# The product with w_spatial as a 2x2 block product of seven products

## Chip, cores and metric

One core of one Trainium2 chip runs the whole program. The metric is the device time of one execution in microseconds; the median of several runs is compared.

## The reference, cut to what matters

Local-plus-summary attention makes x (4 batches, 768 positions, 512 features). Then, per batch:

```python
h = np.maximum(x @ w_in, 0.0)                    # 512 -> 1024
u, v = h[..., :512], h[..., 512:]
v_n = (v - mean(v)) / sqrt(var(v) + 1e-6)        # over the 512 features
v_s = einsum('ts,bsd->btd', w_spatial, v_n) + b_spatial[None, :, None]   # 768 x 768 by 768 x 512
out = (u * v_s) @ w_out                          # 512 -> 512
```

## The kernel before

All products are float32 in three passes: every operand is split into a high and a low float32r part, and `mm3` (line 572) issues, for each block of 128 of the sum, high by high, high by low and low by high, all into one PSUM tile.

Per batch there are these stages, with the names that the profile shows. Attention: `s` (scores), softmax on VectorE (line 478) and ScalarE (482), sums of its rows (line 486) and their reciprocal, `t` (transposes), `x` (mix with v). `proj_v` (`pv`, six tiles of 128 positions; normalised, then split into `vnh` and `vnl`), `proj_u` (`pu`, eight tiles, kept in one `u` buffer), `spatial` (`sp`), `proj_out` (`po`, six tiles, out through `ob`). The attention of the next batch is laid between the dense stages of the present one.

`spatial(b, th, d)` makes one tile of the product: 128 features of v by 512 (`th` = 0) or 256 (`th` = 1) positions, six steps of `mm3`, so 18 matmuls. Then VectorE adds the bias `brep` out of PSUM (line 640), VectorE or GpSimd multiplies by `u` (641), the result is split into high and low (`gt`, `gu`; cast in line 268, subtraction in line 649). The split weight lies in `wsp_h` and `wsp_l` for the whole run, and `po` of four tiles comes between the `th` = 0 and `th` = 1 blocks.

Weights are loaded and split in the first 90 us. The u half of `w_in` has staging of its own: c = 0 and 1 in the place of `u`, c = 2 and 3 in quarters in the `g` places. `wsp_h` lies in the place `wsh`, after `vn`, which holds v of batch 0 for its block sums (`vsums`) and is read last by GpSimd's copy in line 418.

`Plan` gives each operation a place and an engine. An operation that lists several engines (`two_ns`: VectorE or GpSimd) gets one of them. `ORDER` is a written list of all operations with their engines, and each engine runs its part of the list in that order, SyncE's queue of transfers too (line 262). A transfer that waits for a place holds up all that stand behind it in that queue. Up to 110 us of the plan's time each GpSimd operation waits for the last VectorE operation marked `port` that stands before it in the list.

Of the kernel before, what the change touches and what calls it, by code (L numbers as in the profile page):

```python
# [9 lines left out]
F32 = mybir.dt.float32  # L10
# [29 lines left out]
NG = 10  # L40
# [154 lines left out]
def tile_local_summary_attention_gmlp(ctx: ExitStack, tc: tile.TileContext, qT, kext, vext, vnat, vT, w_in, w_sp, b_rep, w_out, out):  # L195
# [130 lines left out]
    def win_load(half, pri):  # L326
        fs = half * DF
        stages = {}
        for c in range(NC):
            if half == 0 and c >= U_BIG:  # L330
                for o in range(0, DF, TH):
                    st = Buf(moe, [P, 2 * TH], F32, "g", f"wi{half}_{c}_{o}")
                    f = Buf(moe, [P, DF], F32, "e", f"wf{half}_{c}_{o}")
                    cs = slice(fs + o, fs + o + TH)
                    split64(st, 0, f, 0, win_v[:, c, cs], win_h[:, c, cs], win_l[:, c, cs], pri, f"wi{half}_{c}_{o}")
                continue
            if c % 2 == 0:
                tag = ("u", None, "vnl", "vnh")[2 * half + c // 2]
                stages[c // 2] = Buf(big, [P, 3 * 1024], F32, tag, f"wi{half}_{c}")
            st = stages[c // 2]  # L340
# [407 lines left out]
    for b in range(B):  # L748
# [21 lines left out]
        for d in range(NC):  # L770
            piece(4.1, spatial, b, 0, d)
# [173 lines left out]
```

## Time and profile before

| | |
|---|---|
| median of 3 runs | 402.4 us (401.82 to 403.41) |
| profiled execution | 400.33 us, span of its core 398.6 us |
| granted TensorE clock, mean | 0.995 |
| PE busy | 388.1 us (97%), 3573 matmuls |
| DVE, ACT, POOL busy | 268.6 us (67%), 201.0 us (50%), 102.4 us (26%; 132 instructions) |
| moved by DMA | 46.36 MB, mean 116 GB/s |
| chain that ended last, by engine | PE 84%, DVE 5%, DMA 4%, ACT 3% |

PE is TensorE, PEld its weight load, DVE VectorE, ACT ScalarE, POOL GpSimd, SP SyncE. Times run from the start of the span. Matmuls are pipelined: the duration that a row shows for one is longer than its distance to the next.

### The profile page before, as it was taken

To read this page: it belongs to the slowest core of one execution; us is meant where nothing else is said; L and a number is where in the kernel's file an instruction comes from. 1 tells how busy PE (TensorE), PEld (TensorE's weight loads), DVE (VectorE), ACT (ScalarE), POOL (GpSimd) and SP (SyncE) were. 2 spreads that over 40 slices of the span, in tenths; PEclk is the share of its full clock that TensorE was granted. 3 is DMA by queue.
4 is the path that set the end of the run, shared out by engine and by line. 5 is a ranking of instruction groups with operands and counts; after the bars stand their busy time and mean duration, and the time that the engine had idled before them with its cause. 6 is when DMAs were issued, how large, how long until landed. Compare 5 with 4: busy or idle time off the path is not lost.

```text
span 398.6 us, 9455 instructions
## 1 busy us (share of the span) xinstructions
PE 388.1 (97%) x3573; PEld 329.6 (83%) x3573; DVE 268.6 (67%) x942; ACT 201.0 (50%) x668; POOL 102.4 (26%) x132
## 2 busy tenths in 40 slices
PE   8699999999999999999999999999999999999996
PEld 8377788887988888898888889888888888888895
DVE  3799999999894988794646657764873535626431
ACT  3599998498273575723615644453734351211101
POOL 4035564520300123222541103331140223300000
PEclk9899999999999999999999999999999999999999
DMA  7987898451334671513247423005012120000022
GB/s 263 398 267 192 277 272 246 140 152 45 95 113 110 238 209 56 146 37 104 76 121 254 109 87 73 2 27 126 10 28 80 40 68 30 0 2 0 0 81 79
DMA packets 22542, 46.36 MB, mean 116 GB/s; under 512 B 2656, under 2 KB 6752, under 8 KB 22368
## 3 DMA queue, kind: packets, MB, share of 16 engines
q1 hardware_dynamic: 22352, 45.62, 37.4%
q8 instruction: 28, 0.46, 0.5%
q14 instruction: 18, 0.15, 0.1%
q10 hardware_dynamic: 144, 0.13, 0.1%
HBM read 39.45 MB, written 6.29 MB: 115 GB/s over the span
## 4 chain that ended last, share of the span: by engine, by line
PE 84%; DVE 5%; DMA 4%; ACT 3%; POOL 1%; SPq 1%; issue 1%; POOLq 0%; ACTq 0%; DVEq 0%
PE sp L572 24%; PE pu L572 17%; PE pv L572 15%; PE po L572 15%; PE x L538 5%; PE s L465 5%; DMA qd<-in_qT_dram 3%; PE t L522 2%; DMA k<-in_kext_dram 1%; SPq L262 1%; ACT p L482 1%; DVE p L478 1%; ACT p L493 1%; PE t L514 1%; DVE gm L377 1%
## 5 line engine op out<-in xcount | busy, mean ns | idle before, releaser
L482 ACT ACTIVATE p<-p,sums 128x120 f32<-128x120 f32 x192 | 73.8, 386 | 45.9 <-DVE sums L478 45.5
L572 PE MATMUL sp<-wsp_h,vnh 128*128 128x512 f32 (+1 forms) x192 | 65.7, 342 | 0.1
L572 PE MATMUL sp<-wsp_l,vnh 128*128 128x512 f32 (+1 forms) x192 | 64.6, 337 | 0.0
L572 PE MATMUL sp<-wsp_h,vnl 128*128 128x512 f32 (+1 forms) x192 | 64.6, 336 | 0.0
L478 DVE CUSTOM_DVE_ANT_0 p<-s,mask 128x120 f32<-128x120 f32 x192 | 45.4, 275 | 22.4 <-PE s L465 22.1
L572 PE MATMUL po<-wo_h,gt 128*128 128x512 f32 (+1 forms) x136 | 47.9, 383 | 0.0
L572 PE MATMUL pu<-xh,win_h 128*128 128x256 f32 (+1 forms) x128 | 43.9, 343 | 0.0
L572 PE MATMUL pu<-xh,win_l 128*128 128x256 f32 (+1 forms) x128 | 43.1, 337 | 0.0
L572 PE MATMUL pu<-xl,win_h 128*128 128x256 f32 (+1 forms) x128 | 43.1, 336 | 0.0
L641 POOL TENSOR_TENSOR g<-g,u 128x256 f32<-128x256 f32 (+1 forms) x18 | 17.7, 992 | 89.7 <-DVE g L640 59.8
L572 PEld LDWEIGHTS sp<-wsp_h,vnh 128*128 128x128 f32 x192 | 36.4, 189 | 5.3 <-DVE ob L268 0.5
L572 PEld LDWEIGHTS sp<-wsp_h,vnl 128*128 128x128 f32 x192 | 36.4, 189 | 3.9
L572 PEld LDWEIGHTS sp<-wsp_l,vnh 128*128 128x128 f32 x192 | 36.4, 190 | 3.8
L572 PE MATMUL po<-wo_l,gt 128*128 128x512 f32 (+1 forms) x100 | 38.2, 382 | 0.0
L572 PE MATMUL pv<-win_h,xh 128*128 128x512 f32 x96 | 37.9, 395 | 0.0
L572 PE MATMUL pv<-win_l,xh 128*128 128x512 f32 x96 | 37.4, 390 | 0.0
L572 PE MATMUL pv<-win_h,xl 128*128 128x512 f32 x96 | 37.4, 390 | 0.0
L640 DVE TENSOR_TENSOR g<-sp,brep 128x512 f32<-128x512 f32 (+1 forms) x32 | 17.6, 554 | 29.2 <-PE sp L572 24.1
L482 ACT ACTIVATION_READ_ACCUMULATOR p<-p,sums 128x1 f32 x192 | 36.2, 189 | 0.0
L572 PEld LDWEIGHTS po<-wo_h,gt 128*128 128x128 f32 x136 | 25.1, 188 | 5.5 <-issue 0.5
L493 ACT ACTIVATE p<-p,sums 128x120 f32<-128x120 f32 x80 | 24.6, 384 | 8.6 <-DVE sums L488 8.5
L538 PEld LDWEIGHTS x<-pt,ve 120*64 120x64 f32 x768 | 23.6, 138 | 5.9 <-issue 3.2
(131 smaller groups left out, 776.0 us busy)
## 6 DMA issues: line engine op xcount, KB each, us to landing
k<-in_kext_dram SPq DMA_DIRECT2D x16, 544.0 KB, 5.6
qd<-in_qT_dram SPq DMA_DIRECT2D x24, 256.0 KB, 3.8
ve<-in_vext_dram SPq DMA_DIRECT2D x23, 256.0 KB, 4.2
out_dram<-ob SPq DMA_DIRECT2D x23, 256.0 KB, 2.1
vt<-in_vT_dram SPq DMA_DIRECT2D x24, 192.0 KB, 2.5
wi<-in_w_in_dram SPq DMA_DIRECT2D x6, 512.0 KB, 6.7
ve<-in_vext_dram SPq DMA_DIRECT2D x22, 128.0 KB, 3.1
wo<-in_w_out_dram SPq DMA_DIRECT2D x8, 256.0 KB, 3.7
```

The costliest lines, as they stand in the source:

```text
L262: add(("SP", issue), lambda e: nc.sync.dma_start(out=out_() if callable(out_) else out_, in_=in_() if callable(in_) else in_), pri, w, r, ...
L377: nc.vector.tensor_reduce(out=g[:, 4 * lo:4 * top].rearrange("p (s g) -> p s g", g=4), in_=t[:, lo * SEG:top * SEG].rearrange("p (s c) -> ...
L465: nc.tensor.matmul(out=ps.t[r * QB:(r + 1) * QB, a, i * KW:(i + 1) * KW], lhsT=qt[hs, r, i], rhs=kts[r].t[hs, g * SEG:g * SEG + KW], start ...
L478: add(("DVE", 203), lambda e, i=i, mi=mi: nc.vector.tensor_tensor_reduce(out=pt.t[:, i, :], in0=ps.t[:, a, i * KW:(i + 1) * KW], in1=mask[ ...
L482: add(("ACT", 380), lambda e, i=i: nc.scalar.activation(out=pt.t[:, i, :], in_=pt.t[:, i, :], func=AF.Exp, scale=-1.0, bias=st.t[:, 0, i:i ...
L493: nc.scalar.mul(out=pt.t[:, i, :], in_=pt.t[:, i, :], mul=st.t[:, 0, i:i + 1])
L514: nc.tensor.transpose(out=ps.t[:KW, a, i * P:(i + 1) * P], in_=pts[a].t[:, i, :], identity=ident)
L522: nc.tensor.transpose(out=ps.t[:KW, r, a * CH + i * QB:a * CH + (i + 1) * QB], in_=pts[a].t[hs, i, :], identity=ident[hs, hs])
L538: nc.tensor.matmul(out=ps.t[a * D:(a + 1) * D, r, n * QB:(n + 1) * QB], lhsT=win(buf, n, o), rhs=rhs(n, a, r), start=True, stop=True)
L572: nc.tensor.matmul(out=ps.t[:, :n], lhsT=x, rhs=y, start=(j == i == 0), stop=(j == last and i == 2))
L640: add(("DVE", dve_ns(n)), lambda e: nc.vector.tensor_add(out=g.t[:, :n], in0=ps.t[:, :n], in1=brep[:, ts]), pri, w=[g], r=[ps, "brep"])
L641: add(two_ns(n), lambda e: eng(e).tensor_mul(out=g.t[:, :n], in0=g.t[:, :n], in1=u.t[:, d, ts]), pri, w=[g], r=[u, (u, d, th)], port=True)
```

## The change

Batch 0 keeps its direct product, in tiles of 384 positions instead of 512 and 256. In batches 1 to 3 the weight and v are cut in 2x2 blocks (384 positions or 384 summed positions; 256 features), and the product is made from seven products of blocks and sums of blocks instead of eight products of blocks. `combine` makes the sums of v's blocks and splits them, with the block sums `z` going to `vs`, which lies in `wsh`. `wsp_mix` makes the sums of the weight's blocks once, after batch 0, from a second read of `w_sp`; they go to DRAM (`mixed_w`), as do the plain split blocks from batch 0 (`wsp_keep`, `plain`). `sums_of` issues the seven products; each reads its three chunks of split weight back from DRAM (`tr`) into one of six places `wl` and issues two tiles of 384 positions, nine matmuls each. VectorE adds each product to what it belongs to.

`u`, the sums, the gated tiles and the stages of weights share eleven places `q` of 768 words. The v means of a batch (`vmean`) are read in quarters instead of halves. The u half of `w_in` with c = 0 to 2 is staged in `wsh`, after `vn` and before `wsp_h`. The order of the last tiles is 3, 4, 5, 0, 1, 2. `ORDER` is written anew as a whole.

```diff
-NG = 10
+HALF = S // 2
+NP = NT // 2
+NQ = 11
+VT = 4
...
-    SLOTS = dict(wsh=1, wsl=1, st=2, ..., g=NG, e=3, u=1, vnh=1, vnl=1, ...)
+    SLOTS = dict(wsh=1, wl=NT, st=2, ..., q=NQ, e=3, vnh=1, vnl=1, ...)
...
+    wsp_l = [Buf(big, [P, S], F32R, "wl", f"wsl{c}") for c in range(NT)]
+    plain = dram.tile([3, NP, P, 2, HALF], F32, name="plain")
+    mixed_w = [dram.tile([2, NP, P, 2, HALF], F32, name=f"mixed_w{i}") for i in range(2)]
...
             if c % (2 if half else 3) == 0:
+                stages[0] = Buf(big, [P, 3 * 1024], F32, ("vnl", "vnh")[c // 2], ...) if half else Buf(big, [P, NT * S], F32, "wsh", ...)
...
+    def wsp_keep(c, pri):
+        p, odd = divmod(c, 2)
+        rows = slice(1, 3) if odd else slice(0, 1)
+        cols = S if odd else HALF
+        for w, src, key in ((0, lambda: wsp_h.t[:, c, :cols], [wsp_h]), (1, lambda: wsp_l[c].t[:, :cols], [wsp_l[c]])):
+            dma(plain[rows, p, :, w].rearrange("o q n -> q o n"), ..., cols / 2, pri, w=[f"wt{c}{w}"], ...)
+
+    def wsp_mix(p, pri):
+        r = []
+        for i in range(2):
+            st = Buf(moe, [P, 2, HALF], F32, "q", f"wx{p}_{i}")
+            dma(lambda st=st: st.t.rearrange("q o n -> q (o n)"), wsp_v[2 * p + i], 384, pri, w=[st], r=["db"], ...)
+            r.append(st)
+        for (o, oi), (x, xi), (y, yi) in (((0, 0), (0, 1), (0, 0)), ((0, 1), (1, 1), (0, 1)), ((1, 1), (1, 1), (0, 0)), ((1, 0), (1, 1), (1, 0))):
+            add(two_ns(HALF), lambda e, ...: eng(e).tensor_sub(out=r[o].t[:, oi], in0=r[x].t[:, xi], in1=r[y].t[:, yi]), ...)
+        for i in range(2):
+            h, l = [Buf(big, [P, 2, HALF], F32R, "wl", f"tg{p}_{i}{w}") for w in "hl"]
+            add(dict(ACT=act_ns(S), DVE=one_ns(S)), lambda e, i=i, h=h: copy(e, h.t, r[i].t), ...)
+            add(two_ns(S), lambda e, i=i, h=h, l=l: eng(e).tensor_sub(out=l.t, in0=r[i].t, in1=h.t), ...)
+            for w, src in enumerate((h, l)):
+                dma(mixed_w[i][:, p, :, w].rearrange("o q n -> q o n"), lambda src=src: src.t.bitcast(F32), 384, ...)
...
+    def combine(b, p, v0, v1, pri):
+        vh, vl, vs = s["vh"], s["vl"], s["vs"]
+        z = Buf(moe, [P, S], F32, "q", f"z{b}_{p}")
+        lo, hi = slice(0, TH), slice(TH, DF)
+        for out_, x, y, op in (((z, lo), (v0, lo), (v0, hi), ALU.subtract), ((v0, hi), (v0, hi), (v1, hi), ALU.add),
+                               ((z, hi), (v0, hi), (v0, lo), ALU.subtract), ((z, slice(DF, S)), (v1, lo), (z, hi), ALU.subtract)):
+            add(two_ns(TH), lambda e, ...: eng(e).tensor_tensor(...), ...)
+        for q, v in enumerate((v0, v1)):
+            divide(v, ..., DF, pri)
+        divide(z, lambda: z.t, ..., S, pri)
...
+    def sums_of(b, piece):
+        def product(n, j, src, o, out_, other, minus, pri, key=None):
+            chunks = []
+            for p in range(NP):
+                ch = Buf(big, [P, 2, HALF], F32R, "wl", f"tr{b}_{n}_{p}")
+                dma(lambda ch=ch: ch.t.bitcast(F32), src[o, p], 384, pri - 9, w=[ch], r=need, tag=f"tr{b}_{n}_{p}")
+                chunks.append(ch)
+            for i in range(2):
+                ps = Buf(ps_m, [P, 512], F32, "m", f"sp{b}_{n}_{i}")
+                mm3(ps, HALF, [...chunks[p].t[:, 0], chunks[p].t[:, 1]... for p in range(NP)], pri, ..., early=True)
+                add(("DVE", dve_ns(HALF)), add_up, pri, w=[(out_, i)], r=[ps, out_, ...])
+        step(3.14, lambda pri: product("1", 0, plain, 0, f1, bias(0), False, pri, brk))
+        step(3.14, lambda pri: (product("2", 2, plain, 1, c11, of(f1), ...), gate(b, 0, 0, c11, None, pri)))
+        step(3.14, lambda pri: product("6", 5, mixed_w[1], 1, f1, of(f1), ...))
+        step(3.14, lambda pri: product("7", 4, mixed_w[0], 1, u3, of(f1), ...))
+        step(3.14, lambda pri: (product("5", 1, mixed_w[0], 0, f5, bias(1), ...),
+                                both(f1, f1, f5, ...), both(f5, u3, f5, ...), gate(b, 1, 1, f5, None, pri)))
+        step(3.14, lambda pri: (product("3", 6, plain, 2, f1, of(f1), ...), gate(b, 0, 1, f1, 0, pri), gate(b, 0, 1, f1, 1, pri)))
+        step(3.14, lambda pri: (product("4", 3, mixed_w[1], 0, u3, of(u3), True, ...), gate(b, 1, 0, u3, 0, pri), gate(b, 1, 0, u3, 1, pri)))
...
-        for d in range(NC):
-            piece(4.1, spatial, b, 0, d)
-        for t in range(4):
-            piece(2.72, proj_out, b, t)
-        for d in range(NC):
-            piece(2.16, spatial, b, 1, d)
-        for t in range(4, NT):
+            for c in range(NT):
+                wsp_keep(c, KEEP_AT + c)
+        if b == 0:
+            for y in range(2):
+                for d in range(NC):
+                    piece(3.14, spatial, b, y, d)
+                for t in range(y * NP, y * NP + NP):
+                    piece(2.72, proj_out, b, t)
+            add(two_ns(HALF), lambda e: eng(e).tensor_sub(out=brep[:, HALF:], in0=brep[:, HALF:], in1=brep[:, :HALF]), ...)
+            for p in range(NP):
+                wsp_mix(p, dense[0] + MIX_AT + 4 * p)
+            continue
+        sums_of(b, piece)
+        for t in (3, 4, 5, 0, 1, 2):
             piece(2.72, proj_out, b, t)
```

## Rows read from the trace of the kernel before

**Rows 1.** Windows: busy time (instructions) per engine, granted clock, share of transfer engines, GB/s.
```profile
core 0: us, PE busy (x) PEld busy (x) DVE busy (x) ACT busy (x) POOL busy (x), PEclk, DMA share, GB/s
...
46.50:82.00 35.50, 35.50 (x309) 30.06 (x302) 33.24 (x122) 27.74 (x89) 18.87 (x21) 1.00 0.78 229
128.00:177.00 49.00, 49.00 (x513) 41.89 (x511) 42.36 (x153) 29.55 (x99) 12.09 (x14) 1.00 0.48 141
177.00:217.00 40.00, 39.90 (x350) 33.98 (x343) 24.36 (x99) 15.81 (x64) 13.29 (x12) 1.00 0.42 131
...
353.00:398.60 45.60, 42.41 (x237) 36.98 (x235) 15.77 (x30) 4.59 (x9) 0.74 (x1) 0.99 0.09 35
```

**Rows 2.** Waits of TensorE from 46 us on: total us, times, longest.
```profile
PE x L538 <- DVE pt L268: 0.9, 1, 0.9
PE t L522 <- ACT p L493: 0.6, 1, 0.6
```

**Rows 3.** Timeline of TensorE in batch 3: start us, duration us, instruction.
```profile
367.07 0.40 PE L572 MATMUL sp<-wsp_h,vnh 128*128 128x512 f32 x1
...
371.18 0.28 PE L572 MATMUL sp<-wsp_h,vnh 128*128 128x256 f32 x1
...
374.41 0.40 PE L572 MATMUL po<-wo_h,gt 128*128 128x512 f32 x1
```

**Rows 4.** Groups of instructions by line and shape: busy us, mean ns, idle before.
```profile
L572 PEld LDWEIGHTS sp<-wsp_h,vnh 128*128 128x128 f32 x192 | 36.4, 189 | 5.3 <-DVE ob L268 0.5 <-issue 0.3 <-DVE xh L268 0.2
...
L640 DVE TENSOR_TENSOR g<-sp,brep 128x512 f32<-128x512 f32 x16 | 11.0, 687 | 18.2 <-PE sp L572 17.9
...
L641 POOL TENSOR_TENSOR g<-g,u 128x512 f32<-128x512 f32 x8 | 10.3, 1288 | 34.7 <-DVE g L640 29.7 <-issue 5.0
...
L641 POOL TENSOR_TENSOR g<-g,u 128x256 f32<-128x256 f32 x10 | 7.5, 755 | 55.1 <-DVE g L640 30.1 <-ACT gt L268 24.9
...
L640 DVE TENSOR_TENSOR g<-sp,brep 128x256 f32<-128x256 f32 x16 | 6.6, 421 | 11.0 <-PE sp L572 6.2 <-DMA out_dram<-ob 4.6
...
L268 ACT CAST gt<-g 128x512 fp32r<-128x512 f32 x8 | 5.0, 622 | 25.7 <-DVE g L641 22.5 <-POOL g L641 3.2
```

**Rows 5.** Windows of the first 20 us, columns as in the first group.
```profile
3.00:20.00 17.00, 13.70 (x110) 10.66 (x113) 10.52 (x36) 8.54 (x24) 2.62 (x15) 0.90 1.00 374
10.00:16.00 6.00, 2.70 (x25) 1.35 (x27) 4.45 (x11) 3.20 (x8) 0.87 (x2) 0.98 1.03 398
16.00:18.00 2.00, 2.00 (x23) 1.22 (x16) 0.75 (x5) 0.89 (x4) 0.00 (x0) 0.50 0.92 381
```

**Rows 6.** Issues of transfers: count, KB of one, median us to landing.
```profile
out_dram<-ob SPq DMA_DIRECT2D x23, 256.0 KB, 2.1
...
brep<-in_b_rep_dram SPq DMA_DIRECT2D x1, 384.0 KB, 4.4
```

**Rows 7.** Waits of SyncE's queue: total us, times, longest.
```profile
SPq L262 <- DVE ob L268: 78.0, 7, 48.0
```

**Rows 8.** Timeline of VectorE and GpSimd near 284 us.
```profile
283.92 1.28 POOL L641 TENSOR_TENSOR g<-g,u 128x512 f32<-128x512 f32 x1 [4.97 <-issue]
284.00 1.23 DVE L486 TENSOR_SCALAR sums<-sums 128x5 f32<-128x5 f32 x1
```

**Rows 9.** Groups of VectorE's instructions in 128 to 217 us.
```profile
L486 DVE TENSOR_SCALAR sums<-sums 128x5 f32<-128x5 f32 x13 | 4.6, 358 | 0.6 <-ACT p L482 0.6
```

**Rows 10.** Line 486 over the run: duration min/median/max in ns.
```profile
L486 DVE TENSOR_SCALAR sums<-sums x48: 138/166/1233, 20.8 to 322.8; 128x5 f32<-128x5 f32 x48
```

**Rows 11.** Timeline of GpSimd and TensorE near 51 us.
```profile
50.73 2.58 POOL L324 TENSOR_TENSOR win_l<-wi 128x512 fp32r<-128x512 f32 x2 [1.10 <-issue]
...
53.42 0.47 PE L572 MATMUL pu<-xh,win_h 128*128 128x512 f32 x1
```

More of the change, by code (lines that the diff above doesn't have):

```diff
@@ L336, in win_load @@
                 continue
[L337 to L340, printed above, removed]
+            if c % (2 if half else 3) == 0:
+                stages[0] = Buf(big, [P, 3 * 1024], F32, ("vnl", "vnh")[c // 2], f"wi{half}_{c}") if half else Buf(big, [P, NT * S], F32, "wsh", f"wi{half}_{c}")
+            st = stages[0]
             cs = slice(fs, fs + DF)
-            so = c % 2 * 1536
+            so = c % (2 if half else 3) * 1536
@@ new lines, in wsp_load @@
+        h, l = lambda: wsp_h.t[:, c, :], wsp_l[c]
+        add(dict(ACT=act_ns(S), DVE=one_ns(S)), lambda e: copy(e, h(), st.t), pri, w=[f"ws{c}h"], r=[st, wsp_h], port=True)
+        add(two_ns(S), lambda e: eng(e).tensor_sub(out=l.t, in0=st.t, in1=h()), pri, w=[f"ws{c}l"], r=[st, f"ws{c}h", wsp_h, l], port=True)
+    def wsp_keep(c, pri):
[3 more added lines that the diff above has]
+        for w, src, key in ((0, lambda: wsp_h.t[:, c, :cols], [wsp_h]), (1, lambda: wsp_l[c].t[:, :cols], [wsp_l[c]])):
+            dma(plain[rows, p, :, w].rearrange("o q n -> q o n"), lambda src=src: src().bitcast(F32).rearrange("q (o n) -> q o n", n=HALF), cols / 2, pri,
+                w=[f"wt{c}{w}"], r=[f"ws{c}{'hl'[w]}", *key], tag=f"wk{c}_{w}")
@@ L438, in vmean @@
         plan.tag = f"vm{b}"
-        add(("PE", 130), lambda e: nc.tensor.transpose(out=ps.t[:, :P], in_=vs_in, identity=ident), pri, w=[ps], r=[f"vs_{pr}_{hf}" for pr in range(NPAIR) for hf in range(2)])
+        add(("PE", 130), lambda e: nc.tensor.transpose(out=ps.t[:, :P], in_=vs_in, identity=ident), pri, w=[ps], r=[f"vs_{pr}_{hf}" for pr in range(NPAIR) for hf in range(VT)])
         for pr in range(NPAIR):
@@ new lines, in spatial @@
+    def spatial(b, y, d, pri):
+        s = batch_state(b)
+        x, i = divmod(d, 2)
+        ps = Buf(ps_m, [P, 512], F32, "m", f"sp{b}_{y}_{d}")
+        plan.tag = f"sp{b}_{y}_{d}"
+        ts = slice(y * HALF, (y + 1) * HALF)
+        ds = slice(d * P, (d + 1) * P)
+        vh, vl = s["vh"], s["vl"]
+        if i == 0:
+            s["raw", x, y] = Buf(moe, [P, 2, HALF], F32, "q", f"c{b}_{x}{y}")
+        raw = s["raw", x, y]
+        mm3(ps, HALF, [((lambda k=k: vh.t[:, k, ds], lambda k=k: vl.t[:, k, ds], lambda k=k: wsp_h.t[:, k, ts], lambda k=k: wsp_l[k].t[:, ts]),
+                        [vh, vl, (vh, k), (vl, k), f"ws{k}h", f"ws{k}l", wsp_h, wsp_l[k]]) for k in range(NT)], pri)
+        plan.tag = f"ge{b}_{y}_{d}"
+        add(("DVE", dve_ns(HALF)), lambda e: nc.vector.tensor_add(out=raw.t[:, i], in0=ps.t[:, :HALF], in1=brep[:, ts]), pri, w=[(raw, i)], r=[ps, "brep", raw])
+        gate(b, x, y, raw, i, pri)
@@ L808 @@
 ON_PE = (0, 1, 2, 3)
-U_BIG, PAIRED_FROM, AFTER = 2, 6, 8.0
+PAIRED_FROM, AFTER = 6, 8.0
+KEEP_AT, MIX_AT = 90.0, 2.0
 SHIFT = {}
```

269 lines of the change are left out of this document (156 added, 113 removed).

## The prediction

> **What bounds the kernel now.** I read the stage table first. From 46.5 us to the last store TensorE is busy for the whole of nearly every stage, while VectorE is at 42.36 of 49 us in 128 to 177 and far below that later [rows 1]. A busy TensorE need not be a paced one, so I read its waits from 46 us on: two, 0.9 and 0.6 us [rows 2]. From 46.5 us on the time is therefore the sum of TensorE's own work plus 1.5 us, and a cut of that work is a cut of the time as long as the other engines and the queue keep up. The third view is the timeline of one stretch of `sp` in batch 3, which gives the price of a matmul by its distance to the next, not by its modelled duration. 18 matmuls of 512 columns run from 367.07 to 371.18 us, so 228.3 ns each; 27 of 256 columns from 371.18 to 374.41 us, so 119.6 ns each [rows 3]. That is 0.4246 ns per column and a fixed 10.9 ns. A weight load lasts 189 ns [rows 4], longer than 119.6, and yet does not set the distance: it is overlapped.
>
> **The change part by part, TensorE.** Before, a batch's product with `w_spatial` is 4 blocks of 18 matmuls at 512 and 18 at 256 columns: 72 x 228.3 + 72 x 119.6 ns = 25.05 us. After, in batches 1 to 3, it is seven products of two halves of nine matmuls with 384 columns: 126 matmuls. By the line above one costs 10.9 + 384 x 0.4246 = 173.9 ns, a product 3.13 us, a batch 21.92 us. Saved: 3.13 us a batch, **9.4 us** in all. Batch 0 goes from 72 + 72 to 144 of 384 columns, 25.05 us, no change. Were a 384-column matmul held to the 189 ns of a weight load, a batch would be 23.8 us and the saving 3.7 us; the 119.6 ns speak against that. No other TensorE work is added, as every sum of blocks is made on VectorE, ScalarE or GpSimd.
>
> **Chunk reads.** Each product needs three chunks of 128 x 768 words, 393 KB, in one of six `wl` places, so two products' chunks are held. A chunk's place comes free when the second half of its product has used it, 2.09, 2.61 and 3.13 us into the product, and the product after the next begins at 6.26: 4.17 us for the first. What a chunk costs is bounded by two rows. In 3 to 20 us the transfer engines were full and moved 374 GB/s [rows 5]: 1.05 us a chunk, 3.15 us for three against a product's 3.13, so even. Latency: `brep`, the same shape, landed 4.4 us after its issue in a crowded stretch, a 256 KB store 2.1 us after [rows 6]. At 4.4 us the first chunk of products 3 to 7 is 0.23 us late, 5 x 0.23 x 3 = 3.5 us in all; at the other end nothing. Batches 1 and 2 share the queue with the next batch's loads, as `brep` did, so I take the crowded end there, cut by the attention blocks between products, and nothing in batch 3, whose stretch has a share of 0.09 [rows 1]: **+1.5 us**, bounds 0 and 3.5.
>
> The chunk reads wait on TensorE in SyncE's queue, and behind them stand the `qd`, `k`, `ve`, `vt` loads of the next batch and the stores of `ob`. That queue already waits long, 78.0 us in all for `ob` [rows 7], and TensorE did not pay for it after 46 us. What would be late next is a load of the attention, then its scores, then TensorE.
>
> One rule speaks against the change here. The Trainium skill, DMA: Bandwidth & Descriptors, Specifications, puts what HBM gives one core at about 358 GB/s; an estimate by it is 1.10 us a chunk, 3.30 us for three, 0.17 us late per product, 0.8 us a batch, and 1.0 us more on the sum. The 374 GB/s of this trace are above that figure, so the row decides.
>
> **Added vector work.** By the rows per shape [rows 4] VectorE pays 687 ns for a two-input operation of 512 columns and 421 for 256, so 1.04 ns a column: 554 ns for 384, 953 for 768. GpSimd: 1288 and 755, so 1.02 us for 384 and 1.82 for 768. A ScalarE cast of 512 columns is 622 ns, so one of 768 at most 0.93 us.
> The mix of weight blocks, once: 12 subtractions of 384 and 6 of 768, 12.4 us on VectorE or 23.2 on GpSimd, and 6 casts, 5.6 us on ScalarE. `combine`, each batch: 12 operations of 256 and 3 of 768, 7.9 us or 14.5, and 3 casts, 2.8 us. The additions out of PSUM: 14 x 554 against 4 x (687 + 421) ns, +3.3 us a batch, VectorE alone; the two wide sums, 1.9 us or 3.6. The gate keeps its columns, the split of `u` and the quarters of `vt` add about 1 us. Without the mix that is some 14 us a batch, in stages where VectorE has 15.6 to 29.8 us free [rows 1]; there I cost it at nothing, and the cover is those free stretches.
> The exception is 128 to 177 us, where the mix and batch 1's `combine` fall: 20.3 us if VectorE takes all, with 6.6 free. GpSimd has 36.9 us free, and would need 37.7 for all of it. So they must share, and sharing has a price that the trace shows: at 283.92 us a GpSimd multiplication of 1.28 us begins, VectorE's 5-column operation beside it at 284.00 lasts 1.23 us [rows 8], against a median of 166 ns [rows 10], and the 1.5 us of TensorE's waits come soon after. In 128 to 217 us 13 of these average 358 ns [rows 9], 13 x 192 = 2.5 us lost beside 26 GpSimd instructions [rows 1], 0.1 us for each. With 20 more GpSimd operations this is **+2.0 us**. Bounds: nothing, as ScalarE and the time up to product 6 can also take some, and 13.7 us, if VectorE takes everything. I go by the lower end, since the kernel does hand GpSimd such work: 18 of 32 `g,u` multiplications [rows 4].
>
> **Head and tail.** `wi` columns of the u half, c = 0 to 2, now wait for the place of `vn`; before, c = 2 had its own places. The first `pu` started at 53.42 us, 0.1 us after the last split on GpSimd ended [rows 11]. So lateness would be paid: at most one 512-column chain of four VectorE operations, priced like `g` at 687 ns, 2.7 us. That chain also replaces two of 256 columns, 8 x 421 ns, 0.6 us less. **+0.3 us**, bounds -0.6 and 2.7. At the end, three `po` blocks now come between the last product's gate and the blocks that need it, 36 x 228.3 ns = 8.2 us, so nothing is added. The two old waits may go or stay: **-0.3 us**, bounds -1.5 and 0. The DRAM writes (8.3 MB) lie in 85 to 170 us, where the queue is about half free [rows 1]: nothing, unless the second rival holds.
>
> **Sum.** -9.4 + 1.5 + 2.0 + 0.3 - 0.3 = -5.9 us. The profiled execution took 400.33 us (span 398.6), so 394.4; the median of the runs is 2.1 us above it, so **396.5 us**.
>
> **The rivals.**
> *Full saving* (15%): chunks and sums all hidden, -9.4 to -8.5: 393.5 us. For it: no wait was paid in 128 to 177 with VectorE at 86%.
> *VectorE binds in batch 1* (12%): the mix and `combine` go mostly to VectorE, or GpSimd's share blocks it. With 60 to 90% of the 20.3 us on VectorE the stage overruns by 5.6 to 11.7 us; with the chunks' 1.5 that makes 400.1 to 406.2 us, centre 402.5, no change that can be told. For it: the collision of [rows 8]; against it: ScalarE has 19 us free there. The Trainium skill, SBUF — State Buffer, SBUF: two separate sides, calls the port pair that VectorE and GpSimd share an exclusive lock held for the whole instruction; by that rule the row at 284 us is the normal case.
> *The transfers bind* (13%), the case on the slow side: chunks queue behind `ve` and `k` and move as in 46.5 to 82 us, 229 GB/s at a share of 0.78, so 294 GB/s [rows 1] and 1.34 us a chunk. Three are 4.02 us against 3.13, 5 x 0.89 = 4.4 us a batch, 13.3 in all: -9.4 + 13.3 + 2.0 = +5.9, 408.3 us. It decides from 1.25 us a chunk on: 15 x (3.75 - 3.13) = 9.3 us eats the saving. In batch 1 the present loads fill 0.42 of 40 us; with 15 chunks at 1.05 us that is 32.6 of 36.9 us, at 1.34 all of it. Longer gaps may cost clock too: after a sparse TensorE in 10 to 16 us (2.7 of 6 us busy) the granted clock read 0.50, the 1.2 GHz level, in 16 to 18 us [rows 5].
> Against it: the 374 GB/s of [rows 5].
>
> **How the numbers follow.** Half a per cent, 2 us, is about what a measurement of this kernel can tell from no change. My forecast (57%, 394 to 399.5 us, the stalls between 1 and 6.5 us) and the full saving are faster; the VectorE case is mostly the same; the transfers are slower; 3% stay for a late head. Faster 0.72, same 0.13, slower 0.15. The range, 392 to 403.5 us, leaves out the transfers and the far end of the VectorE case, and below it what would need the old waits gone as well.
>
> **What would show it.** Right: 126 `sp` matmuls a batch at about 174 ns from one to the next; TensorE's waits from 46 us on at some 5 us in all, most of them in batch 1; VectorE above nine tenths in 120 to 175 us; chunk reads landing in 3 to 4.5 us. Wrong: TensorE waiting for `tr` reads for over 3 us a batch (transfers), for attention's ScalarE or VectorE work for over 6 us in batch 1 (VectorE), or `pu` starting after 56 us (head). The prediction fails most easily on the chunk's landing and on how much of batch 1's sums VectorE takes.

## The result, and the profile of the changed kernel

The changed kernel takes 403.51 us, median of 20 runs, against 401.02 us for the kernel before, median of 20 runs beside it: a ratio of 1.0057, 95% interval 1.0040 to 1.0075. By the ratio it is slower by some 2.3 us, where 396.5 us were forecast. One of the 20 runs (408.41 us), and one or two of the runs with own stages and with the head order below, fell in a slower state; the ratios leave them out. Its profiled execution took 405.33 us (span 403.6), 5.0 us more than that of before and 1.8 us above its own median.

The matmuls do what was forecast. The timeline of TensorE in batch 3 (start us, duration us, instruction) answers to [rows 3]:

```profile
372.05 0.51 PE L596 MATMUL sp<-tr,vnh 128*128 128x384 f32 x2
372.39 0.33 PE L596 MATMUL sp<-tr,vnl 128*128 128x384 f32 x1
372.56 0.51 PE L596 MATMUL sp<-tr,vnh 128*128 128x384 f32 x2
...
374.64 0.51 PE L596 MATMUL sp<-tr,vnh 128*128 128x384 f32 x2
```

From 372.05 to 374.64 us go 15 matmuls, 172.7 ns each; 173.9 were forecast. So the 9.4 us of TensorE's work did go. What came instead is seen in the stages, with the columns of [rows 1]:

```profile
46.50:85.40 38.90, 38.07 (x364) 32.45 (x363) 34.16 (x127) 34.44 (x106) 18.69 (x19) 1.00 0.73 233
130.00:180.00 50.00, 47.45 (x364) 39.02 (x364) 41.71 (x131) 31.46 (x98) 25.36 (x26) 1.00 0.83 271
180.00:210.50 30.50, 28.87 (x289) 26.25 (x288) 21.88 (x57) 12.10 (x31) 8.21 (x6) 1.00 0.80 255
357.00:403.60 46.60, 41.88 (x232) 38.23 (x231) 20.30 (x31) 7.83 (x15) 7.33 (x6) 0.99 0.47 161
```

TensorE, full in these stages before, now has 2.55 us free in the second and 1.63 in the third. VectorE is no fuller than before in batch 1's stage (0.83 of it, 0.86 before); GpSimd took the added work, 25.36 us in place of 12.09. The transfer engines went from a share of 0.48 to 0.83. TensorE's waits from 46 us on (total us, times, longest), two rows in [rows 2], are now headed by

```profile
PE sp L596 <- DMA tr<-mixed_w: 2.2, 3, 1.2
PE sp L596 <- DMA tr<-plain: 1.9, 5, 0.5
PE po L596 <- ACT ob L274: 1.2, 1, 1.2
PE t L538 <- POOL p L519: 0.8, 1, 0.8
```

The page's issues of transfers (count, KB, median us to landing), beside [rows 6], point to the reason for the first two: a chunk takes as long as `brep` did in the crowd, and longer.

```profile
tr<-mixed_w SPq DMA_DIRECT2D x36, 384.0 KB, 5.0
tr<-plain SPq DMA_DIRECT2D x27, 384.0 KB, 4.9
```

A wait is named in a trace only where it is long enough to be told from the pace of the matmuls, so I compared lengths as well: when TensorE starts batch 0's first `sp` (81.6 us before, 85.4 after), and how long the stretch from first to last `sp` lasts in batches 1 to 3. The changed kernel and all its variants keep one order of TensorE's steps behind the head, so these stretches hold the same work in each.

| kernel | median us | ratio to before (95%) | first `sp` | stretch of batch 1, 2, 3 |
|---|---|---|---|---|
| changed | 403.51 | 1.0057 (1.0040 to 1.0075) | 85.4 | 30.6, 31.8, 26.8 |
| tiny chunks | 397.75 | 0.9900 (0.9863 to 0.9936) | 83.8 | 29.2, 30.4, 25.3 |
| nine places | 399.15 | 0.9951 (0.9928 to 0.9974) | 86.5 | 28.5, 30.5, 24.6 |
| k places | 401.80 | 0.9995 (0.9972 to 1.0017) | 86.6 | 31.3, 31.6, 24.6 |
| all vector work narrow | 401.18 | 0.9976 (0.9946 to 1.0007) | 85.3 | 31.0, 30.5, 27.0 |
| weight sums narrow | 401.90 | 1.0024 (1.0003 to 1.0045) | 82.0 | 31.1, 32.0, 25.8 |
| vn early | 405.40 | 1.0101 (1.0064 to 1.0137) | 85.7 | 32.4, 31.2, 27.0 |
| own stage | 404.28 | 1.0050 (1.0018 to 1.0082) | 84.9 | 31.3, 34.5, 25.7 |
| own stage, vn early | 403.37 | 1.0075 (1.0049 to 1.0102) | 85.2 | 32.1, 32.0, 26.2 |
| the same, k places | 401.32 | 1.0008 (0.9977 to 1.0038) | 85.4 | 31.5, 32.2, 24.6 |
| head order | 402.11 | 1.0033 (1.0006 to 1.0060) | 84.6 | 30.5, 31.7, 26.8 |
| head order, longer | 404.21 | 1.0082 (1.0051 to 1.0113) | 86.1 | 31.1, 31.7, 26.0 |
| head order, k places | 400.57 | 0.9982 (0.9957 to 1.0007) | 85.4 | 32.2, 31.1, 24.6 |
| head order, k and spare places | 400.69 | 0.9984 (0.9962 to 1.0005) | 85.0 | 33.0, 30.8, 24.6 |
| the same, spare places read early | 406.17 | 1.0104 (1.0064 to 1.0144) | 84.4 | 35.2, 35.0, 24.5 |
| busy wait 18 | 404.42 | 1.0077 (1.0048 to 1.0106) | 85.3 | 31.5, 31.6, 26.5 |
| busy wait 18, k places | 401.95 | 1.0020 (1.0000 to 1.0041) | 84.1 | 32.0, 32.6, 24.6 |
| **busy wait 9, k places** | **399.55** | **0.9965 (0.9940 to 0.9990)** | 83.0 | 31.6, 32.3, 24.5 |

Starts and stretches are those of one profiled execution each; a single stretch varies by 1 us or more, a first `sp` too (below). The kernel before ran beside each of them and its median moved between 400.79 and 401.41 us, so where a difference of medians and one of ratios disagree below, the ratios are the safer of the two.

### The profile page after: what moved, and what is told of

The parts are those of the page before. It is cut to its first block, busy times and chain, and to the rows that moved or that the text cites. A ratio compares the mean times of both kernels' runs of the same rounds, so it can differ in the third digit from the quotient of the medians.

```text
span 403.6 us, 9645 instructions
## 1 busy us (share of the span) xinstructions
PE 384.9 (95%) x3521; PEld 332.9 (82%) x3521; DVE 300.3 (74%) x1001; ACT 219.1 (54%) x696; POOL 120.2 (30%) x141
## 4 chain that ended last, share of the span: by engine, by line
PE 56%; DMA 20%; DVE 13%; ACT 5%; POOL 2%; issue 2%; SPq 1%; POOLq 0%; ACTq 0%
PE sp L596 15%; PE po L596 12%; PE pu L596 8%; PE pv L596 8%; DMA tr<-mixed_w 5%; PE x L562 5%; PE s L489 4%; DMA vt<-in_vT_dram 4%; DMA tr<-plain 4%; DMA vn<-in_vnat_dram 3%; DMA wi<-in_w_in_dram 2%; PE t L546 2%; DMA k<-in_kext_dram 2%; DVE p L502 1%; DVE mv L628 1%
## 5 line engine op out<-in xcount | busy, mean ns | idle before, releaser
L506 ACT ACTIVATE p<-p,sums 128x120 f32<-128x120 f32 x192 | 74.0, 388 | 34.6 <-DVE sums L502 34.5
L596 PE MATMUL pu<-xh,win_h 128*128 128x512 f32 (+1 forms) x128 | 44.0, 344 | 0.9 <-DVE vf L280 0.5
L596 PE MATMUL pu<-xl,win_h 128*128 128x512 f32 (+1 forms) x128 | 43.1, 337 | 0.0
L596 PE MATMUL pu<-xh,win_l 128*128 128x512 f32 (+1 forms) x128 | 43.1, 336 | 0.0
L596 PE MATMUL sp<-tr,vnh 128*128 128x384 f32 x144 | 37.7, 342 | 2.1 <-DMA tr<-plain 0.9
L596 PE MATMUL po<-wo_h,gh 128*128 128x512 f32 (+1 forms) x100 | 38.6, 386 | 1.2 <-ACT ob L274 1.2
L596 PE MATMUL po<-wo_h,gl 128*128 128x512 f32 (+1 forms) x100 | 38.2, 382 | 0.0
L596 PE MATMUL po<-wo_l,gh 128*128 128x512 f32 (+1 forms) x100 | 38.1, 381 | 0.0
L596 PE MATMUL sp<-tr,vs 128*128 128x384 f32 x162 | 31.7, 342 | 3.2 <-DMA tr<-mixed_w 2.2
L596 PEld LDWEIGHTS sp<-tr,vs 128*128 128x128 f32 x162 | 27.7, 188 | 5.5 <-DMA tr<-mixed_w 2.4
L278 ACT ACTIVATE u<-pu 128x384 f32<-128x384 f32 (+2 forms) x39 | 14.3, 391 | 32.8 <-PE pu L596 32.7
L562 PE MATMUL x<-pt,ve 120*64 120x64 f32 x768 | 26.3, 224 | 0.9 <-issue 0.4
```

The lines of the kernel that those rows point to most:

```text
L278: nc.scalar.activation(out=out_, in_=in_, func=AF.Relu)
L506: add(("ACT", 380), lambda e, i=i: nc.scalar.activation(out=pt.t[:, i, :], in_=pt.t[:, i, :], func=AF.Exp, scale=-1.0, bias=st.t[:, 0, i:i ...
L562: nc.tensor.matmul(out=ps.t[a * D:(a + 1) * D, r, n * QB:(n + 1) * QB], lhsT=win(buf, n, o), rhs=rhs(n, a, r), start=True, stop=True)
L596: nc.tensor.matmul(out=ps.t[:, :n], lhsT=x, rhs=y, start=(j == i == 0), stop=(j == last and i == 2))
```

## The experiments

Expectations speak of 4.3 us lost in batch 3 and of 6.5 us over batches 1 to 3. They came from counting matmuls in windows, and are too large: the trace holds all 126 `sp` matmuls of batch 3, and the stretches above put its loss at 26.8 - 24.6 = 2.2 us.

### The chunks: bytes, or places

**Tiny chunks.** Every read shrinks from 384 to 16 KB.

```diff
-dma(lambda ch=ch: ch.t.bitcast(F32), src[o, p], 384, ...)
+dma(lambda ch=ch: ch.t[:, 0, :32].bitcast(F32), src[o, p][:, 0, :32], 384, ...)
-lambda ch=chunks[p]: ch.t[:, 0], lambda ch=chunks[p]: ch.t[:, 1]
+*[lambda ch=chunks[p]: ch.t[:, 0, :32].unsqueeze(1).broadcast_to([P, 12, 32])] * 2
```

> The changed kernel with each of its 63 chunk reads cut to 32 columns (16 KB instead of 384 KB); the matmuls read these 32 columns twelve times over, so that they have as many columns as before. Left out: most of the weight sums' data, so the products of batches 1 to 3 are not the reference's. Every wait, place and instruction stays. Theory A (landing and transfer time of the chunks cost about 6.5 us over batches 1 to 3, 4.3 of it in batch 3): 396.5 to 398, and the 3.6 us of lost time between 360 and 376 us gone. Rival B (the added vector work makes the sp matmuls late): 402 or more, and the sp rows still wait for DVE, ACT or POOL. Rival C (the order of TensorE's steps itself, or the matmuls at 384 columns): 403.

397.75 us, 5.8 below the changed kernel (6.3 by the ratios, 1.6 either way), inside theory A's 396.5 to 398; TensorE's waits name no read any more. The chunk reads cost some 6 us. Whether it is their bytes or the time that they take does not follow, since both went.

**Nine places.** Bytes stay.

```diff
-SLOTS = dict(wsh=1, wl=NT, ...
+SLOTS = dict(wsh=1, wl=9, ...
-wo_l = const.tile([P, NC, DM], F32R, name="wo_l")
+wo_l = wo_h
-mask = const.tile([P, 3, KW], F32, name="mask")
+mask = const.tile([P, 1, KW], F32, name="mask")
```

> The changed kernel with nine chunk places instead of six in all batches; the space comes from w_out's low-order half, which shares the high-order half's tile, and from two of the three attention masks. Left out: w_out's low-order half and two masks, so the result is not the reference's. Bytes, order of issue and number of instructions in batches 1 to 3 stay. Theory A (a chunk's place comes free one product before it is needed, 3.1 us, and the read takes 4.9 us): the same gain as with tiny chunks in batches 1 to 3, 4 to 6 us, 397.5 to 399.5. Rival R (the transfer rate binds: 21 chunks need more than the 21.9 us of a batch's seven products): at most 2 us, 401.5 or more. Rival Q (chunk reads stand in SyncE's queue behind vt reads that wait for VectorE, and not for places): batches 1 and 2 keep their loss, batch 3 loses under 1 us, 401 to 402.

399.15 us, 4.4 below (4.3 by the ratios, 1.2 either way). The three stretches sum to 83.6 us against 89.2, even less than with tiny chunks (84.9). The reads themselves were no quicker, by the page's issues of this kernel:

```profile
tr<-mixed_w SPq DMA_DIRECT2D x36, 384.0 KB, 5.3
tr<-plain SPq DMA_DIRECT2D x27, 384.0 KB, 5.1
```

What shrank is SyncE's wait for places that `sp` still uses (total us, times, longest; the changed kernel, then this one):

```profile
SPq L268 <- PE sp L596: 33.7, 35, 5.3
SPq L268 <- PE sp L596: 13.7, 14, 3.9
```

So rival R, a rate that binds whatever the places, falls, and so does Q as a cause by itself: the same bytes in the same queue order are hidden once a read can start one product earlier.

**k places.** A version of this that computes everything: eight of batch 3's chunks go to the k tiles, idle by then.

```diff
-ch = Buf(big, [P, 2, HALF], F32R, "wl", f"tr{b}_{n}_{p}")
+ch = Buf(*((att, [P, 2, HALF], F32R, "k") if f"tr{b}_{n}_{p}" in IN_K
+           else (big, [P, 2, HALF], F32R, "wl")), f"tr{b}_{n}_{p}")
```

> The changed kernel with eight of batch 3's 21 chunks in the four places of the k tiles, which nothing uses by then: ten chunks instead of six can be read before its first product. Bytes, order of issue and results stay. Theory A (batch 3 loses 4.3 us because a chunk's place comes free too late for the 4.9 us that a read takes to land): 2.5 to 4 us below the changed kernel, 399.5 to 401; the lost time between 360 and 376 us under 1 us. Rival (batch 3 loses its time to the vector work behind each product, or to the order of steps): within 1 us of 403.5.

401.80 us, 1.7 below (2.5 by the ratios, 1.1 either way), at or under the low end of what was expected: batch 3 had only 2.2 us to give, and gave all of them. Three windows of batch 3, first of the changed kernel, then of this one, columns as in [rows 1]:

```profile
360.00:364.00 4.00, 3.61 (x22) 3.19 (x21) 2.46 (x4) 1.11 (x2) 0.00 (x0) 1.00 0.91 283
364.00:368.00 4.00, 4.00 (x24) 4.00 (x25) 1.67 (x3) 0.00 (x0) 1.65 (x1) 1.00 0.82 264
368.00:372.00 4.00, 3.47 (x20) 3.15 (x19) 0.83 (x2) 0.00 (x0) 0.19 (x1) 1.00 0.97 331
```

```profile
360.00:364.00 4.00, 4.00 (x26) 3.91 (x25) 2.51 (x4) 1.11 (x2) 0.00 (x0) 1.00 0.90 289
364.00:368.00 4.00, 4.00 (x25) 4.00 (x24) 1.51 (x4) 0.00 (x0) 1.85 (x1) 1.00 0.89 269
368.00:372.00 4.00, 4.00 (x25) 4.00 (x24) 1.36 (x3) 0.00 (x0) 0.00 (x0) 1.00 1.00 304
```

At much the same rate, 293 and 287 GB/s over these 12 us, TensorE is held up in the first and not in the second. A share of transfer engines near 1.00 is thus no proof that TensorE waits: what counts is whether the data were asked for early enough. The rate still matters. The products use three chunks in 3.13 us, 377 GB/s, more than any of these windows moved; ten places cover the gap with chunks read ahead. In this kernel 11 of batch 3's 21 chunks are asked for after its first `sp`, in the changed one 15. More places thus both start a read earlier and leave fewer to be read in the stretch, and these runs do not tell the two apart.

**Spare places in batches 1 and 2.** On top of the head order and the k places (both below), three chunks a batch go to places of the `q` ring that the written order leaves free there; then their reads are moved ahead too.

```diff
+IN_Q = ("tr1_6_1", "tr1_7_2", "tr1_6_0", "tr2_2_2", "tr2_7_0", "tr2_6_1",)
+ch = Buf(*(... (moe, [P, 2, HALF], F32R, "q") if name in IN_Q else ...), name)
```

> The run with the head order and the k places, and three chunks each of batches 1 and 2 in places of the q ring that are free in that stretch (by the written order 7 to 8 of its 11 are in use when they are read). Results, bytes and order of issue stay. Places theory: the chunk stalls of batches 1 and 2 shrink as those of batch 3 did (sp stretch of batch 1 from 32.2 to 30 us, of batch 2 from 31.1 to 30), 1 to 3 us below the run without them, 398 to 399.5, faster than the kernel before by 0.4 to 0.7%. Rival Q (in batches 1 and 2 the reads stand in SyncE's queue behind vt reads that wait for VectorE, so more places give nothing): within 0.7 us of 400.6.

> As the run with spare places, and the three reads that go to them are issued right behind the sixth read of their batch, ahead of the vt, v and qd reads that stood between. Rival Q with places as a second condition: only now does the stall of batches 1 and 2 shrink, 397.5 to 399. Places theory alone: the same as without the move, within 0.7 us. Against the move: the attention reads that it pushes back (v, h and vt of the next batch) are late in their place, 400 or more.

400.69 us, no gain over 400.57: in these batches the free places alone do not help, as rival Q had it. Read early, it is 406.17 us, and TensorE's waits from 46 us on name another owner:

```profile
PE sp L596 <- DVE f L739: 4.1, 1, 4.1
PE sp L596 <- DVE u L280: 3.4, 1, 3.4
```

`sp` no longer waits for chunks (0.3 us) but 7.5 us for VectorE. That the reads pushed back (`vt`, `v`, `h`) are what VectorE was held by is argued, not shown. Batches 1 and 2 keep their loss of about 3.4 us in a kernel that computes everything.

### The vector work

> The changed kernel with its added vector work narrowed to 8 columns an instruction (4 in the two sums of products): the four sums and the third split per pair of v tiles, the four differences and the two splits per pair of w_spatial rows (the DRAM writes then take the raw rows), the two sums of products. The third product set reads the plain v tiles. Left out: the values of all these, so the result is not the reference's; instructions, waits and transfers stay in number and size. Rival B (vector work costs more than the 2.0 us of the prediction and is what TensorE waits for in 120 to 180 us and in batch 3): 398.5 to 400, idle of TensorE in 120 to 180 us down from 4.6 to about 1. Theory A (chunks and head carry the loss, vector work 0.5 to 1.5 us): 402 to 403.

```diff
-eng(e).tensor_sub(out=r[o].t[:, oi], in0=r[x].t[:, xi], in1=r[y].t[:, yi])
+eng(e).tensor_sub(out=r[o].t[:, oi, :8], in0=r[x].t[:, xi, :8], in1=r[y].t[:, yi, :8])
-divide(z, lambda: z.t, ...
+divide(z, lambda: z.t[:, :8], ...
```

and likewise the other instructions named. 401.18 us, 2.3 below (3.2 by the ratios, 1.4 either way): between the two theories, and no less than the 2.0 us of the prediction's term.

> The changed kernel with only the vector work on the weight sums narrowed to 8 columns an instruction (twelve differences, six splits; the DRAM writes take the raw rows); the work on v and on the products stays. Left out: the values of the weight sums. All added vector work together was worth 2.3 us in the medians. If the weight sums, 18 instructions per launch between the sp stages of batches 0 and 1, are most of it: 401 to 402. If the sums of v tiles and products in each of three batches are: 403 to 403.5.

The same edit for the weight sums alone: 401.90 us, 1.6 below (1.3 by the ratios, 1.1 either way): in the range for "most of it" by the medians, less than half of 3.2 by the ratios, so the split is open.

Nor do the traces show where this time was paid. The weight sums and batch 1's `combine` lie between batch 0's last `sp` and batch 1's first. From the one to the other TensorE took 50.5 us in the changed kernel's profiled execution, 48.0 with all the vector work narrow, 46.8 with the weight sums narrow, and 46.8 again in the run with 18 small matmuls below, which has all of the work (VectorE busy 40.73 us there, GpSimd 24.86) and TensorE busy throughout. So all of the added work can fit in this stage without a wait of TensorE.

### The head

The first `sp` is 3.8 us later in the changed kernel's profiled execution. I read the chain of waits there: SyncE issues `vn` at 11.12 us (5.26 before), TensorE waits for it until 24.03, and the reads of `w_in` that share its place are issued from 26.98 on. Four runs took away one or both.

```
reads, changed:   ... q0_0_0 k0_2 wi1_1 k0_3 wi0_3_0 q0_0_1 vn q0_1_0 vt h0_0 vt wi0_0 q0_1_1 wi0_2 ...
vn early:         ... q0_0_0 vn k0_2 wi1_1 k0_3 wi0_3_0 q0_0_1 q0_1_0 vt h0_0 vt wi0_0 ...
own stage:        ... q0_0_0 k0_2 wi1_1 k0_3 wi0_3_0 q0_0_1 wi0_0 vn q0_1_0 vt h0_0 wi0_2 wi0_1 vt ...
```

> The changed kernel with one load moved: SyncE issues vn right behind the first qd, as the kernel before did (5.26 us there, 11.12 us in the changed kernel). Nothing else in the written order moves. Theory A (the head loses its 3.8 us because vn is issued 5.9 us later, so that the vsum matmuls wait 2.3 us for it and TensorE stays at its lower clock over 10 to 30 us): first sp of batch 0 from 85.5 back to 82 to 83 us, time 3 to 4 us below the changed kernel, 399.5 to 400.5. Rival (the staging of w_in in wsh, as the prediction had it, or the loads that vn now pushes back): first sp stays within 1 us of 85.5, time within 1 us of 403.5.

> The changed kernel with blocks 0 to 2 of the u half of w_in staged in the six chunk places, which are idle in the head, in place of the tile that they share with vn: each block is read and split in two halves of 256 columns (21 more instructions), and their reads are issued ahead of the first vt read that waits, not behind vn's last use. vn stays where the changed kernel has it. Results stay. Theory H (the head's 3.8 us come from these reads: they wait for vn's last user, are issued at 27 to 28 us, land at 33, and ScalarE's conversion of them stands ahead of attention's work): first pv from 36.2 to 33.5 to 34.5 us, first sp from 85.4 to 82 to 83.5, time 2 to 3 us below the changed kernel, 400.5 to 401.5. Rival V (vn's late landing alone keeps the head late, so that freeing the stage gives nothing while vn stays at 11 us): within 1 us of 403.5. Rival S (the smaller splits cost what the earlier reads give): 403 or more.

> As the run with the stages in chunk places, and vn's load issued behind the first qd as well. Results stay. Theory H with both causes (vn late and the stage behind vn each hide the other, which is why vn alone gave nothing): first sp at 81.5 to 83, time 3 to 4 us below the changed kernel, 399.5 to 400.5. Rival (one of the two is the whole cause): the same time as the run without vn's move, within 0.7 us. Rival (the head is late for vector work that neither touches): 403.

> The two head edits together with the k places for eight of batch 3's chunks. Results stay. If head and batch 3 are separate losses, their gains add: the head's 3 to 4 us and 1.7 to 2.5 us in batch 3 give 397.5 to 399 us, 2 to 3.5 us below the kernel before. If the gains hide each other (the same idle time given back later), it is no faster than either alone: 400 or more.

405.40, 404.28 and 403.37 us, and 401.32 with the k places: none of the head edits gained, and my reading of the chain fell twice. With `vn` early the wait for it is gone and TensorE's waits to 46 us are others:

```profile
PE s L489 <- DMA qd<-in_qT_dram: 2.1, 2, 1.6
...
PE s L489 <- ACT k L414: 1.4, 1, 1.4
PE wwi L316 <- DVE win_l L306: 1.1, 1, 1.1
```

The reads that `vn` overtook are needed as soon. Until 20 us the transfer engines are full in either kernel (a share of 1.03 from 10 to 20 us in the changed one, 1.00 from 3 to 20 in [rows 5]); a read moved up moves another down.

**Head order.** So the next runs took over the kernel before's order of reads, vector work and TensorE's steps together, for its first 186 and 237 operations.

> The changed kernel with stages of w_in in the chunk places, and the kernel before's written order for the first 186 operations (loads, vector work and TensorE's steps up to the transposes of the second pair of heads; vt reads stay quarters); from there on the changed kernel's order. Results stay. Theory O (the head is bound by its loads to 20 us and by VectorE and ScalarE from 20 to 55 us; the kernel before fills the wait for vn and qd with the first w_in blocks' vector work, the changed kernel's order can't, and moved loads alone change nothing because their vector work stays late): first sp from 85.4 to 82 to 83.5 us, idle of VectorE in 25 to 30 us from 2.4 to under 0.5, time 2 to 3.5 us below the changed kernel, 400 to 401.5. Rival F (the head's loss is forced by the places: vt in quarters in one place, stages split in halves): first sp at 84.5 or later, 403 or more.

> The same head order, and the four k places for eight of batch 3's chunks. Results stay. Theory O and the places theory together: 2 us for batch 3 and 2 to 3.5 us for the head, 397.5 to 399.5 us, faster than the kernel before by 0.4 to 0.9%. Rival F: as with k places alone, 401 to 402.

> As the run with the head order, but with the kernel before's order for the first 237 operations, up to the second pair's mixing matmuls. Theory O: at least as early as with 186 operations, first sp 81.5 to 83. Rival (the seam between the two orders, not their content, decides): the two cuts differ by more than 1 us, and the later cut may be the slower one.

402.11, 400.57 (with k places) and 404.21 us. Up to 36 us TensorE runs as it did before (first `pv` at 32.8 us; 33.0 before, 36.2 in the changed kernel). By the first `sp` 2.6 of these 3.4 us are lost again, in 36 to 50 us, where one order gives way to the other (TensorE stands idle for 1.4 us of 40 to 46 us). The cut matters, as the rival of the last run said; whether a head planned as a whole keeps the gain is open.

**The clock.** Then the run with narrow weight sums, whose head is the changed kernel's to the instruction, started its first `sp` at 82.0 us. Its timeline and window around `vsum`, after those of the changed kernel (start, duration, instruction; columns as in [rows 1]):

```profile
24.03 2.77 PE L433 MATMUL vsum<-vn,vs_one 128*24 128x128 f32 x48 [2.31 <-DMA vn<-in_vnat_dram]
...
24.00:27.00 3.00, 2.97 (x56) 2.27 (x60) 2.71 (x14) 2.42 (x8) 1.03 (x1) 0.51 0.15 44
```

```profile
22.80 1.51 PE L433 MATMUL vsum<-vn,vs_one 128*24 128x128 f32 x48 [2.08 <-DMA vn<-in_vnat_dram]
...
24.20:27.00 2.80, 2.80 (x53) 2.60 (x49) 1.96 (x7) 2.67 (x10) 0.00 (x0) 1.00 0.56 122
```

TensorE stands idle for `vn` in both. In the one its granted clock then reads 0.51, the 1.2 GHz level, and the same 48 matmuls take 2.77 us; in the other it stays at 1.00, and they take 1.51. The Trainium skill, TensorE: Matmul & The Clock Gate, HAM oscillation, describes just that: a wait for transfers in the middle of a kernel lets the clock drop to half. The trace agrees, though not in every execution. The two differ by more than the clock, since `vn` also landed 1.2 us earlier in the second. Six of the traces have this head, and three more have it with the small matmuls that come below (times in us):

| kernel | wait for `vn` | `vsum` starts, lasts | end of `vsum` to first `pv` | first `sp` |
|---|---|---|---|---|
| changed | 2.31 | 24.03, 2.77 | 9.40 | 85.4 |
| tiny chunks | 2.60 | 23.11, 1.79 | 10.58 | 83.8 |
| nine places | 2.81 | 23.71, 2.77 | 10.65 | 86.5 |
| k places | 3.52 | 23.95, 2.77 | 10.56 | 86.6 |
| all vector work narrow | 3.41 | 23.98, 2.77 | 10.15 | 85.3 |
| weight sums narrow | 2.08 | 22.80, 1.51 | 9.31 | 82.0 |
| busy wait 18 | filled | 25.97, 1.51 | 9.31 | 85.3 |
| busy wait 18, k places | filled | 24.68, 1.51 | 9.31 | 84.1 |
| busy wait 9, k places | filled | 23.80, 1.51 | 9.31 | 83.0 |

In the first five the granted clock read 0.50 to 0.53 in 24 to 27 us, in the other four 1.00. With the clock at 1.00 the first `pv` comes 9.31 us behind `vsum`, each time; with the low clock `vsum` and what follows take 1.4 to 2.6 us longer. That much of the head is the clock. The rest goes with the late landing of `vn`, which no run isolates. Nor is a full clock enough: with `vn` early it read 1.00 from 10 to 30 us, and the first `pv` still came at 36.9. Why one execution of the six kept its clock is open. Over 20 runs the changed kernel's mean granted clock was 0.993; that of the kernel before, over 25 runs, 0.996.

The last four runs keep TensorE at work during the wait.

```diff
-for _ in range(int((...) * WARM)):
+for _ in range(int((...) * WARM) + (9 if op.tag == "vs" else 0)):
     nc.tensor.matmul(out=warm.t[:, :KW], lhsT=ident, rhs=ident[:, :KW], start=True, stop=True)
```

> The changed kernel with 18 more of its small matmuls on the identity (128x120, some 2.3 us in all) ahead of the vsum matmuls, so that TensorE works while it waits for vn. Nothing else moves; results stay. Theory C (the wait for vn, 21.5 to 24.0 us, lets TensorE's granted clock fall to 0.50 in 24 to 27 us, vsum takes 2.8 us and not 1.4, and the vector chain behind it starts late; an execution in which the clock stayed at 1.00 had its first sp at 82.0): granted clock 1.00 from 20 to 30 us, first sp at 82 to 83, mean clock of the executions 0.996 or more, 1.5 to 3 us below the changed kernel, 400.5 to 402. Rival (the head is late for its loads and vector work, and the clock only follows): first sp at 85 or more, 403 to 404.

> As the run with the busy wait, with the k places for eight of batch 3's chunks. Results stay. Theory C and the places theory: 1.5 to 3 us and 1.7 to 2.5 us are separate, 398.5 to 400, faster than the kernel before by 0.3 to 0.7%. Rival to C: as with k places alone, 401.8.

> The kernel before with 18 more small matmuls ahead of its first scores, where TensorE waits 2.5 us for qd and its clock is 0.66 in 15 to 20 us. Results stay. If theory C holds in general, the kernel before gains from it too: 0.5 to 1.5 us, 399.5 to 400.5. If its wait costs nothing behind it (the vector work of the softmax sets the pace): 400.5 to 401.3.

> The k places and nine of the small matmuls ahead of vsum in place of 18. The 18 took 4.5 us, some 0.22 us each, and held vsum back to 26.0 and 24.7 us in the two runs that had them; nine take 2.0 us, inside the wait of 2.3 to 3.5 us. Results stay. Theory C (low clock behind the wait): clock near 1.00 from 20 to 30 us, vsum at 22.8 to 24.2 and 1.4 us long, first sp at 82 to 84, 399.5 to 401. If the head's lateness is the time at which vn lands and the loads behind it, with the clock a small part: first sp at 84 or more, 401 to 402.

With 18, the clock stays at 1.00 and the time is no better, 404.42 us, 401.95 with the k places: I had sized them at half their price. The timeline of the first:

```profile
21.54 4.50 PE L902 MATMUL warm<-ident 128*128 128x120 f32 x38
25.97 1.51 PE L433 MATMUL vsum<-vn,vs_one 128*24 128x128 f32 x48
```

They hold `vsum` back by 2 us, for which a full clock does not make up. The kernel before, with 18 ahead of its first scores, takes 401.11 us beside 400.79: nothing gained there either, and its first scores start 1.5 us later, an overshoot again. Nine fit the wait:

```profile
21.38 2.49 PE L902 MATMUL warm<-ident 128*128 128x120 f32 x20
23.80 1.51 PE L433 MATMUL vsum<-vn,vs_one 128*24 128x128 f32 x48
...
20.00:25.00 5.00, 5.00 (x99) 4.61 (x101) 5.00 (x34) 4.97 (x18) 1.70 (x2) 1.00 0.59 172
```

399.55 us, 2.2 below the k places alone (1.2 by the ratios, 1.3 either way, so not clear of noise), at a mean granted clock of 0.997 against 0.992. Over the 190 runs of the changed kernel and its variants, each compared with its own kernel's mean, 0.001 of granted clock goes with 0.25 us, so 0.005 with 1.3 us: the clock fits the gain, which is not the same as being shown. This version computes everything and is faster than the kernel before by 0.35%, 0.1 to 0.6. It is the only one of the thirteen variants of the changed kernel with whole results whose interval lies below 1, and the best of thirteen is helped a little by luck.

## Why the prediction was wrong, point by point

The forecast stands on 402.4 us, a median of 3 runs; 20 runs give 401.02. What is to be explained is thus a change of +2.3 us where -5.9 was forecast.

**TensorE's saving, -9.4 us: right**, at 172.7 ns a matmul.

**Chunk reads, +1.5 us: the step that failed most**; they cost 4.4 us (nine places) to 5.8 us (tiny chunks) by the medians, 4.3 to 6.3 by the ratios, above the upper bound of 3.5. The mechanism was named rightly, a place free 4.17 us before it is needed. The size went wrong three times. The rate of [rows 5], 374 GB/s and 1.05 us a chunk, did not hold: in 360 to 372 us the transfers moved 293 GB/s, 1.34 us a chunk, where a product leaves 1.04. Landing takes 4.9 to 5.0 us, not the 4.4 of one read: by the prediction's own formula, 0.73 to 0.83 us late per product, 11 to 12 us for 15 products, of which about half was seen (argued: a late product also moves the next need back). And I cut the term to less than half of its bound, with "nothing in batch 3" because the transfer engines' share was 0.09 there. That share was the old kernel's; the reads bring their own load, and batch 3 lost 2.2 us at a share of 0.82 to 0.97. The estimate that I made there from the Trainium skill, DMA: Bandwidth & Descriptors, Specifications, about 358 GB/s, would have given 0.8 us a batch; these windows moved less than that, and batch 3 lost more.

**The rival "transfers bind"** had the right wait and, at 1.34 us a chunk, the right rate. What it had wrong is that every product pays for it. It put 4.4 us on each batch; batch 3 lost 2.2 of these, and none with ten places, at a rate as low.

**Added vector work, +2.0 us: right in size, in part by luck** (2.3 by the run that narrows all of it, 3.2 by the ratios). That it is mostly the weight sums is not settled, and the stage where I put it ran once at TensorE's full pace with all of the work in it. The mark that I gave was wrong: VectorE did not go above nine tenths in batch 1, GpSimd took the work. The rival "VectorE binds" did not occur.

**Head, +0.3 us: the second step that failed.** I priced the staging of `w_in` and looked no further; giving it its own place changed nothing, and my mark for a late head, `pu` after 56 us, was not reached (54.85). I did not price that `vn` is issued 5.9 us later, nor that TensorE's idle wait for it is followed by the low clock. The first `sp` came 3.8 us late in the profiled execution, the first `pv` 3.2; 1.4 us of that is the clock, up to 2.6 in other executions. Nine small matmuls gained 1.2 us by the ratios, not clear of noise.

**The old waits and the tail, -0.3 us**: nothing in the runs speaks for more.

Put together on the profiled executions, +5.0 us: -9.4, +3.8 in the head, +5.6 in the three stretches (89.2 against 83.6) and +3.8 between batch 0's last `sp` and batch 1's first (50.5 against 46.8, the least of any variant) make +3.8; 1.2 us is left unassigned. The 50.5 is this execution's own (46.8 to 48.4 in the others), and probably most of the 1.8 us by which it lies above its median.

## What to carry to other kernels

When resident data is replaced by data read back in pieces, count places by time: landing, issue and use together must fit in the turns that the places give, with the landing that such reads will have in their own crowd. A full transfer engine and a late read look the same in a profile; more places at the same bytes show whether asking earlier is enough. Where a load moves behind others in the head, look at what TensorE does while it waits, and fill the wait with no more work than it holds.

## What the runs showed of the hardware

- Landing of a 384 KB read: median 4.9 to 5.3 us with several under way; the first read of the changed kernel's batch 3 that found the transfer engines idle (issued at 358.90 us) took 3.1. The Trainium skill, DMA: Bandwidth & Descriptors, Anatomy of one DMA, fits a lone one (on GpSimd's path) with 2.0 us and bytes over 436 GB/s; an estimate by it is 2.9 us, near that first read. For reads in a crowd the rows decide.
- A wait for `vn` of 2.1 to 3.5 us, in the same instructions, was followed by a granted clock of 0.50 to 0.53 in five executions and of 1.00 in one; the half clock cost `vsum` up to 1.26 us. The first `sp` of two of them differ by 3.4 us, of which 1.2 is `vn`'s earlier landing and 1.3 `vsum`.
- A small float32 matmul of 120 columns takes 0.22 us in a row and is counted as two records: 38 records (19 of them) last 4.50 us, 20 records 2.49.
